# Moving small attention products between the runs of an attention and SwiGLU kernel, sharing row copies between two engines, and taking a statistic in steps

## The chip, the cores and the metric

The kernel runs on one core of one Trainium2 chip. The metric is the device time of one execution in microseconds (us), the median of several. A core has a matrix engine (TensorE, PE in the profile, with its weight loads shown apart as PEld), a vector engine (VectorE, DVE), an activation engine (ScalarE, ACT), a general engine (GpSimd, POOL), and a sync engine (SyncE, SP) that here only issues DMAs. Each engine runs its own instructions in order and waits for others by semaphores. PE writes to accumulators in PSUM, eight banks here, each a tile of 128 x 512 numbers of 32 bits; DVE and ACT read them, POOL doesn't.

## The reference

A linear attention without softmax for 8 batches, 8 heads, 576 rows and 64 columns per head, then a SwiGLU network on its 4608 rows of 512:

```python
kv = einsum('bhsd,bhse->bhde', k, v)              # 64 x 64 per batch and head
o = einsum('bhsd,bhde->bhse', q, kv)
o = o / sqrt(mean(o * o, -1) + 1e-6) * g_norm
x = o.transpose(0, 2, 1, 3).reshape(B * S, H * D)  # 4608 x 512
xn = x / sqrt(mean(x * x, -1) + 1e-6) * rms_g
g, val = xn @ w_gate, xn @ w_val                   # 512 -> 1536
out = (silu(g) * val) @ w_out                      # 1536 -> 512
```

Inputs and output are 32-bit floats; the kernel multiplies in bfloat16 and accumulates in 32 bits.

## The kernel before, in words

The rows are cut into nine groups of 512. Groups 0 to 7 are the first 512 rows of batches 0 to 7. Group 8 holds the remainders, the last 64 rows of each of the eight batches. Groups go through the network in the order 0 to 6, 8, 7.

A group g from 1 on takes 40 slots. The first 24 alternate a gate (`gate_of`) and a value (`val_of`) for each of 12 blocks of hidden units: four multiplies of 512 columns each into a tile of the PSUM pool mm1 (`mm1`, L762). ACT takes the silu of the gate (L771), DVE multiplies it by the value (L783). The last 16 slots are the output multiplies (L811), three in each, into the pool o2; ACT copies the sums (L831) and SP stores them. Pools: mm1 has 3 tiles, o2 has 2, att has 3. A new tile waits until the last reader of its predecessor in the same bank is done.

While PE does the network of one group, the attention of the next batch is placed between its slots. For batch b this is `place_attention`, in the slots of group b - 1. It has a run of k-v products (`kv_mm`, L294, 40 multiplies on 128 rows by 64 columns of the array, into one tile of att), two DVE copies into `kvs` (`kv_half`, L324), and a run of o (`o_heads`, L422, 32 multiplies on 64 rows by 128 columns, into two tiles of o2 and two of att). ACT takes squares and copies of o (`sq_`, `outa_`), POOL weights the squares with g_norm (`wsq`, L514), DVE sums them (`red`, L522), computes the scale per row and head in a chain of 12 small instructions (`chain`), and applies it (`xna_`). SP then turns the result into the layout of x with two transposing DMAs (`x_dma`, L653).

K-v products of 4 and 5 share one run, and those of 6 and 7 (`mate`). The remainders' o comes in pairs of batches (`o_rem`, L397, 16 multiplies on quarters of the array, 64 by 64): batches 0 and 1 in the run of o of batch 2, 2 and 3 with 3, 4 and 5 with 5, 6 and 7 with 7. It is written to half a tile of att and half a tile of mm1, read by four ACT instructions 256 wide (`sq_rem` L405, `outa_rem` L410), goes through the same chain as the fifth chunk, and its transposing DMA fills a part of `xr`, the x of group 8.

Where an operation goes is decided when the program is made. `Placer.put` gives each operation the first slot that its inputs and the engine's estimated backlog allow: `ROOM` is what an engine has free in a slot, `BEHIND` how far it may fall back, and costs are written at each call. `Placer.psum` adds that the tiles of att used before have been read. `start` and `chain_at` are slots that an operation may not precede. In a slot the operations of other engines are issued first, then the slot's own work, then the placed PE operations. The order of the tiles fixed there decides what each engine queues behind what.

Batches 0 and 1 are written out by hand. Batch 0 has no work to hide in: group 0 starts with the first 256 of its rows. `early` lists its slots (gates 0 to 2, then values 0 to 2, gates 3 to 5, values 3 to 5, gates 6 to 8, values 6 to 8), and `behind(n)` what follows slot n for the last 256 rows. `behind(4)` issues products of values 0 to 2 that had been held back (`held`); `behind(9)`, after value 5, has eight PE transposes (L621) and four copies of their rows to x on ACT (`xT_out`, L631; the DVE form of the same copy is L633). The first gate over the last 256 rows is the slot after gate 8. Batch 1 is in `place_second`: four transposed products of k-v with q (`oT_mm`, L472) into att, their squares on ACT (`sqT_`, L483), and sixteen small multiplies that sum the squares over a head (`stat_mm`, L507), which a DVE chain reads (`lead_chain`, L539 and on).

POOL issues the loads of k and v, which cast to bfloat16 on the way (`load_cast`): per batch and tensor a main piece (L200) and a remainder (L196). Batch 2's are the last of a long line behind the weights. SP issues the loads of q from batch 2 on, and the transposing DMAs of q (`qT_dma`).

Of the kernel before, what the change touches and what calls it, by code (L numbers as in the profile page):

```python
# [87 lines left out]
def kernel(  # L88
# [12 lines left out]
    nc = tc.nc  # L101
# [25 lines left out]
    xna_p = pool("xna", 2)  # L127
    x_p = pool("x", 3)
# [30 lines left out]
    q01r = consts.tile([2 * REM, H, D], BF16, name="q01r")  # L159
# [29 lines left out]
    def load_cast(b, t, heads=None):  # L189
        to = qc if t == 0 else (vc if t == 2 else kc)[b % 2]  # L190
        if heads is None:
            if t == 0:
                to = q01r[b * REM : (b + 1) * REM]
            else:
                to = to[:REM, :, NC * D :]
            return nc.gpsimd.dma_start(  # L196
                out=to, in_=src[t][b, :, MAIN:S, :].rearrange("h p d -> p h d")
            )
        view = src[t][b, :, 0:MAIN, :].rearrange("h (p c) d -> p h (c d)", c=NC)[:, heads[0] : heads[1]]
        return nc.gpsimd.dma_start(out=to[:, heads[0] : heads[1], : NC * D], in_=view)  # L200
# [62 lines left out]
    class Att:  # L263
        def __init__(self, b):
            self.b = b
            self.kv, self.qT = kvs[b % 2 if b else 2], qTs[b % 2]
            self.chunks = NC + (b == 2 or b > 2 and b % 2)
            if b < 2:
                self.qTj = self.qT.rearrange("p c j t -> p (c j t)").rearrange("p (j c t) -> p j c t", j=NS, c=NC + 1)
# [51 lines left out]

        def kv_half(self, half):
            rows, cols = slice(half * D, (half + 1) * D), slice(half * D, (half + 1) * D)
            nc.vector.tensor_copy(out=self.kv[rows, :, half, :], in_=self.kv_ps[rows, :, cols])  # L324
# [54 lines left out]
        def qT_dma(self):  # L379
            flat = mains[self.b, 0].rearrange("p c h d -> p (c h d)")  # L380
            nc.sync.dma_start_transpose(out=self.qT[:, 0:NC].rearrange("p c j t -> p (c j) t"), in_=flat)
            if self.chunks > NC:
                rem = q01r if self.b == 2 else rems[0][self.b // 2 % 2]
                nc.sync.dma_start_transpose(out=self.qT[:, NC], in_=rem.rearrange("p h d -> p (h d)"))

        def o_rem(self):

            of = (kvs[2], kvs[1]) if self.b == 2 else (kvs[0], kvs[1])
            self.o[NC] = [
                pool_.tile([128, H // 2, D], FP32, name=name) for pool_, name in ((att_p, "att"), (mm1_p, "mm1"))  # L390
            ]
            for j in range(NS):
                for n in range(2):
                    at = slice(n * REM, (n + 1) * REM)
                    for half in range(2):
                        rows = slice(half * D, (half + 1) * D)
                        nc.tensor.matmul(  # L397
                            self.o[NC][half][at, j, :], lhsT=self.qTj[rows, j, NC, at],
                            rhs=of[n][rows, j, half, :], start=True, stop=True, skip_group_check=True,
                        )  # L400

        def sq_rem(self, half):
            if NC not in self.sq:
                self.sq[NC] = sq_p.tile([128, 2, H, D], BF16, name="sq")
            nc.scalar.activation(out=self.sq[NC][:, 0, half:H:2, :], in_=self.o[NC][half], func=ACT.Square)  # L405

        def outa_rem(self, half):
            if NC not in self.outa:
                self.outa[NC] = outa_p.tile([128, H, D], BF16, name="outa")
            nc.scalar.copy(out=self.outa[NC][:, half:H:2, :], in_=self.o[NC][half])  # L410

        def o_heads(self):
# [5 lines left out]
            for c in range(NC):  # L418
                for j in range(NS):
                    for half in range(2):  # L420
# [3 lines left out]
                            rhs=self.kv[rows, j, half, :], start=True, stop=True, skip_group_check=True,  # L424
# [4 lines left out]
        def part(self, t, n):  # L429

            if n >= NC:
                return t[:, n]
# [12 lines left out]
        def xna_pairs(self, o, js, c0, c1):  # L445
            if not hasattr(self, "xna"):
                self.xna = xna_p.tile([128, NC + 1, H, D], BF16, name="xna")
# [6 lines left out]
        def o_of(self, c):  # L454
            return self.o[c] if c >= NC else self.o["main", c].rearrange("p c h d -> p (c h) d")
# [47 lines left out]
        def stat_mm(self, c0, c1):  # L503
            self.st = st = att_p.tile([128, 2, NC + 1, H], FP32, name="att")
            for c in range(c0, c1):
                for j in range(NS):
                    nc.tensor.matmul(  # L507
                        st[:, :, c, 2 * j : 2 * j + 2], lhsT=self.sqT[:, j, c], rhs=sel,
                        start=c == c0 and j == 0, stop=c == c1 - 1 and j == NS - 1,
                        skip_group_check=True,  # L510
                    )

# [3 lines left out]
        def red(self, c, which):  # L516
            if self.st is None:
                self.st = stat.tile([128, 2, NC + 1, H], FP32, name="st")
            of = self.sq[c][:, which]
            if c < NC:  # L520
                of = of.rearrange("p (c h) d -> p c h d", c=2)
            nc.vector.reduce_sum(out=self.part(self.st[:, which], c), in_=of, axis=AX.X)  # L522

        def chain_t(self):
            if not hasattr(self, "al"):
                t = lambda n, dt=FP32, h=H: stat.tile([128, NC + 1, h], dt, name=n)
                self.u, self.r, self.t, self.z, self.nt, self.al = (t(n) for n in ("u", "r", "t", "z", "nt", "al"))
                self.s = stat.tile([128, NC + 1], FP32, name="srow")
# [57 lines left out]
        def xna_(self, c, eng):  # L586
            if not hasattr(self, "xna"):
                self.xna = xna_p.tile([128, NC + 1, H, D], BF16, name="xna")
            if c < NC:
                of = self.o["main", c] if self.b == 1 else self.outa[c].rearrange("p (c h) d -> p c h d", c=2)  # L590
                return eng.tensor_tensor(  # L591
                    out=self.part(self.xna, c), in0=of,
                    in1=self.part(self.al, c).to_broadcast([128, 2, H // 2, D]), op=OP.mult,
                )
            return eng.tensor_tensor(
                out=self.xna[:, c], in0=self.outa[c], in1=self.al[:, c, :].to_broadcast([128, H, D]), op=OP.mult
# [48 lines left out]
        def x_dma(self, c0, c1):  # L645
# [3 lines left out]
            else:  # L649
                b = self.b // 2 * 2 if self.b > 2 else 0  # L650
                to = xr[:, :, b * REM : (b + 2) * REM]
                of = self.xna[:, NC].rearrange("p h d -> p (h d)")
# [16 lines left out]
    def place_attention(P, b, casts=(), at=0, chain_at=0, mate=None):  # L669
# [3 lines left out]
        N1 = range(a.chunks)  # L673
        P.floor = max(P.floor, at)
        load = P.put("SP", 0.0, a.qT_dma, casts[:1] if b == 2 else casts)
        qt = [("DMA", load[1] + QT_SLOTS)]
        if kv is None:
            of = [a] + ([Att(mate)] if mate else [])
            p = P.psum(1.2, lambda: [o.kv_mm(ALL) for o in of], casts, len(of))
            out_ = [[P.put("DVE", 0.4, lambda o=o, h=h: o.kv_half(h), [p]) for h in range(2)] for o in of]  # L680
            for tile_, ops in zip(P.tiles[-len(of) :], out_):
                tile_ += ops
            kv = out_[0]
            if mate:
                ahead[mate] = of[1], out_[1]
        else:
            P.floor = max(P.floor, start + 2)
        outs, reds = {}, []
        rem = a.chunks - NC
        main = P.psum(0.73 + 0.25 * rem, a.o_heads, kv + qt, 2 + rem)  # L690
        for c in (*N1[NC:], *N1[:NC]):
            if c == NC:
                for n in (1, 0):
# [433 lines left out]
```

## Time and profile before

| What | Value |
|---|---|
| Median of 3 runs | 317.47 us (317.18 to 317.76) |
| The profiled execution's own time | 317.45 us |
| Its span | 315.7 us |
| PE busy | 310.6 us (98%) |
| DVE busy | 167.6 us (53%) |
| ACT busy | 139.1 us (44%) |
| POOL busy | 87.4 us (28%) |
| DMA | 40.18 MB, mean 127 GB/s |

The span runs from the first to the last instruction of the profiled execution; the 1.75 us around it belong to its own time. Times in a profile are from the start of the span. Lines of groups name the line of the kernel, the engine, the operation, output and inputs with shapes, count, busy time and mean ns of one. The chain that ended last is followed back from the last instruction: each piece has a start, a length and what it was. A line of the timeline has a start, a length, the engine, the operation, a count, and in brackets how long the engine had been idle and what ended that; consecutive instructions of one kind are merged. The length of a PE instruction includes the pipeline, so the next starts before it ends; the step from one start to the next is what it costs.

### The profile page before, as it was taken

To read this page: it belongs to the slowest core of one execution; us is meant where nothing else is said; L and a number is where in the kernel's file an instruction comes from. 1 tells how busy PE (TensorE), PEld (TensorE's weight loads), DVE (VectorE), ACT (ScalarE), POOL (GpSimd) and SP (SyncE) were. 2 spreads that over 40 slices of the span, in tenths; PEclk is the share of its full clock that TensorE was granted. 3 is DMA by queue.
4 is the path that set the end of the run, shared out by engine and by line. 5 is a ranking of instruction groups with operands and counts; after the bars stand their busy time and mean duration, and the time that the engine had idled before them with its cause. 6 is when DMAs were issued, how large, how long until landed. Compare 5 with 4: busy or idle time off the path is not lost.

```text
span 315.7 us, 5706 instructions
## 1 busy us (share of the span) xinstructions
PE 310.6 (98%) x2220; PEld 154.8 (49%) x2220; DVE 167.6 (53%) x375; ACT 139.1 (44%) x261; POOL 87.4 (28%) x108
## 2 busy tenths in 40 slices
PE   8999999999999999999999999999999999999996
PEld 3688655544444445444444454444444444444444
DVE  4585456579669643955196638570769034103410
ACT  2374474595487324632483228322842233233321
POOL 8846430077068205830081007100510000000000
PEclk9999999999999999999999999999999999999999
DMA  9999999999899968997423444424001600040002
GB/s 199 194 203 199 196 237 200 192 231 147 190 162 215 179 152 140 253 175 163 166 85 67 94 135 141 83 48 152 3 0 25 194 1 0 21 105 9 2 33 100
DMA packets 78358, 40.18 MB, mean 127 GB/s; under 512 B 43000, under 2 KB 73852, under 8 KB 78332
## 3 DMA queue, kind: packets, MB, share of 16 engines
q0 software_dynamic: 32304, 14.75, 36.5%
q1 hardware_dynamic: 45328, 24.48, 31.6%
q10 hardware_dynamic: 700, 0.59, 0.6%
q8 instruction: 17, 0.28, 0.3%
q14 instruction: 9, 0.07, 0.1%
HBM read 37.78 MB, written 9.44 MB: 150 GB/s over the span
## 4 chain that ended last, share of the span: by engine, by line
PE 94%; DMA 2%; DVE 1%; POOL 1%; issue 1%; ACT 0%; DVEq 0%; POOLq 0%
PE mm L762 58%; PE o L811 27%; DMA vc<-in_v_dram 2%; PE mm L811 2%; PE att L294 2%; PE o L422 1%; PE o L842 1%; PE att L422 1%; PE att L472 1%; DVE h L783 0%; PE att L621 0%; PE mm L804 0%; PE o L762 0%; PE att L397 0%; PE mm L312 0%
## 5 line engine op out<-in xcount | busy, mean ns | idle before, releaser
L783 DVE TENSOR_TENSOR h<-silu,mm 128x512 bf16<-128x512 bf16 (+1 forms) x114 | 73.9, 650 | 101.1 <-PE mm L762 92.4
L771 ACT ACTIVATE silu<-mm 128x512 bf16<-128x512 f32 (+1 forms) x115 | 65.1, 570 | 83.5 <-PE mm L762 73.1
L762 PE MATMUL mm<-x,wv 128*128 128x512 bf16 (+1 forms) x408 | 97.7, 364 | 0.0
L762 PE MATMUL mm<-x,wg 128*128 128x512 bf16 (+1 forms) x404 | 97.5, 364 | 0.1
L811 PE MATMUL o<-wo,h 128*128 128x512 bf16 x396 | 89.6, 379 | 0.0
L762 PEld LDWEIGHTS <-wv 128*128 128x128 bf16 x468 | 45.1, 98 | 46.2
L762 PEld LDWEIGHTS <-wg 128*128 128x128 bf16 x456 | 44.4, 98 | 47.5 <-issue 0.4
L811 PEld LDWEIGHTS <-h 128*128 128x128 bf16 x420 | 40.6, 98 | 47.6
L514 POOL TENSOR_TENSOR sq<-sq,g 128x512 bf16<-128x512 bf16 x28 | 32.0, 1155 | 99.1 <-ACT sq L405 67.4
L831 ACT COPY osb<-o 128x512 f32<-128x512 f32 x33 | 19.3, 587 | 68.7 <-PE o L811 66.7
L522 DVE TENSOR_REDUCE st<-sq 128x8 f32<-128x512 bf16 x56 | 35.9, 678 | 0.0
L591 DVE TENSOR_TENSOR xna<-outa,al 128x512 bf16<-128x512 bf16 x24 | 15.1, 684 | 0.0
L324 DVE CAST kvs<-att 64x256 bf16<-64x256 f32 x14 | 5.9, 422 | 16.8 <-PE att L294 16.6
L200 POOL DMA_DIRECT2D kc<-in_k_dram x7 | 6.5, 924 | 29.0 <-PE att L294 26.1
L762 PE MATMUL mm<-xr,wg 128*128 128x512 bf16 x48 | 12.3, 379 | 0.0
L762 PE MATMUL mm<-xr,wv 128*128 128x512 bf16 x48 | 12.3, 379 | 0.0
L229 POOL CAST main_q<-stg 128x1024 bf16<-128x1024 f32 x10 | 10.1, 1043 | 1.2 <-DMA stg<-in_q_dram 1.2
L929 ACT ACTIVATE wv<-wv,gain 128x384 bf16<-128x384 bf16 x16 | 9.0, 607 | 0.4 <-PE mm L762 0.4
L200 POOL DMA_DIRECT2D vc<-in_v_dram x10 | 8.5, 857 | 2.1 <-PE att L294 1.1
L258 PE MATMUL mm<-idle 128*128 128x512 bf16 x20 | 7.2, 533 | 1.2 <-DVE idle L138 1.2
L811 PE MATMUL mm<-wo,h 128*128 128x512 bf16 x24 | 7.6, 379 | 0.0
L459 ACT ACTIVATE sq<-att 128x512 bf16<-128x512 f32 x12 | 7.5, 626 | 0.0
(151 smaller groups left out, 190.1 us busy)
## 6 DMA issues: line engine op xcount, KB each, us to landing
out_dram<-osb SPq DMA_DIRECT2D x27, 256.0 KB, 2.5
stg<-in_q_dram SPq DMA_DIRECT2D x6, 1024.0 KB, 11.2
vc<-in_v_dram POOLq DMA_DIRECT2D x7, 512.0 KB, 13.1
kc<-in_k_dram POOLq DMA_DIRECT2D x7, 512.0 KB, 7.8
out_dram<-osb SPq DMA_DIRECT2D x17, 128.0 KB, 2.4
wg<-in_moe_w_gate_dram POOLq DMA_DIRECT2D x4, 384.0 KB, 10.1
wv<-in_moe_w_val_dram POOLq DMA_DIRECT2D x4, 384.0 KB, 11.3
wo<-in_moe_w_out_dram POOLq DMA_DIRECT2D x4, 384.0 KB, 14.4
```

Source lines behind the costliest of these rows:

```text
L200: return nc.gpsimd.dma_start(out=to[:, heads[0] : heads[1], : NC * D], in_=view)
L229: return copy(out=mains[b, t][:, cs[0] : cs[1], h0:h1, :], in_=staged[b, t].rearrange("p h (c d) -> p c h d", c=NC)[:, cs[0] : cs[1], h0:h ...
L459: nc.scalar.activation(out=self.sq[c][:, 0], in_=self.o_of(c), func=ACT.Square)
L514: eng.tensor_tensor(out=self.sq[c][:, 1], in0=self.sq[c][:, 0], in1=g2, op=OP.mult)
L522: nc.vector.reduce_sum(out=self.part(self.st[:, which], c), in_=of, axis=AX.X)
L591: return eng.tensor_tensor(out=self.part(self.xna, c), in0=of, in1=self.part(self.al, c).to_broadcast([128, 2, H // 2, D]), op=OP.mult,)
L762: nc.tensor.matmul(ps[:, : c1 - c0], lhsT=w[n][:, s, jj * 128 : (jj + 1) * 128], rhs=x_of(g, s, c0, c1), start=s == 0, stop=s == NS - 1)
L771: nc.scalar.activation(out=sis[g, j][:, c0:c1], in_=ps, func=ACT.Silu)
L783: nc.vector.tensor_tensor(out=hs[g, j][:, c0:c1], in0=sis[g, j][:, c0:c1], in1=v_ps, op=OP.mult)
L811: nc.tensor.matmul(ps, lhsT=hs[g, j][:, t * 128 : (t + 1) * 128], rhs=wo[j // OB][:, j % OB, :], start=j == 0, stop=j == NF - 1)
L831: (eng.copy if eng is nc.scalar else eng.tensor_copy)(out=o, in_=ps)
L929: A.mul(out=w[:, s], in_=w[:, s], mul=gain[:, s : s + 1])
```

## The change

- Batch 0: gate 7 of the first 256 rows takes its tile from o2, not mm1. Of the four row copies in `behind(9)`, the last two go to DVE.
- Batch 1: `stat_mm` is gone. Its sixteen multiplies are four calls of `stat_pairs`, one for each transposed product, in the slots s + 3, s + 4, s + 4 and s + 5; all were in s + 5. Their tile is taken at s + 3.
- K-v: each batch has its own `kvs` tile (from batch 2 on without the zero blocks), and one memset on POOL is dropped. Batch 4's products have a run of their own; those of batch 5 follow o of 4 in its run; those of 6 and 7 follow o of 5 in its run, 6 into att and 7 into mm1.
- Remainders: their q is transposed when it was, but each pair has a tile `qTr` of its own. Their o is computed two pairs at a time: pairs (0, 1) and (2, 3) in the run of o of batch 6, (4, 5) and (6, 7) in that of 7. A tile of att and one of mm1 then hold both pairs, and the squares and copies on ACT are 512 wide, as for the main rows. In batches 6 and 7 the chain is done twice, for the main rows and the remainders (batch 7: remainders first).

The diff, cut to its core:

```diff
-    kvs = [consts.tile([128, NS, 2, D], BF16, name=f"kvs{n}") for n in range(3)]
-    qTs = [consts.tile([128, NC + 1, NS, 128], BF16, name=f"qTs{n}") for n in range(2)]
+    kvs = [consts.tile([128, NS, 2, D] if n < 2 else [128, NS, D], BF16, name=f"kvs{n}") for n in range(B)]
+    qTs = [consts.tile([128, NC, NS, 128], BF16, name=f"qTs{n}") for n in range(2)]
+    qTr = [consts.tile([128, NS, 128], BF16, name=f"qTr{n}") for n in range(B // 2)]
...
-            self.kv, self.qT = kvs[b % 2 if b else 2], qTs[b % 2]
-            self.chunks = NC + (b == 2 or b > 2 and b % 2)
+            self.kv, self.qT = kvs[b], qTs[b % 2]
+            self.rems = {6: (0, 1), 7: (2, 3)}.get(b, ())
+            self.chunks = NC + len(self.rems)
...
-        def kv_mm(self, js):
+        def kv_mm(self, js, pool=None):
             if not hasattr(self, "kv_ps"):
-                self.kv_ps = att_p.tile([128, NS, 2 * D], FP32, name="att")
+                self.kv_ps = (pool or att_p).tile([128, NS, 2 * D], FP32, name="mm1" if pool is mm1_p else "att")
...
         def o_rem(self):
-            of = (kvs[2], kvs[1]) if self.b == 2 else (kvs[0], kvs[1])
-            self.o[NC] = [
-                pool_.tile([128, H // 2, D], FP32, name=name) for pool_, name in ((att_p, "att"), (mm1_p, "mm1"))
-            ]
...
+            for half, (pool_, name) in enumerate(((att_p, "att"), (mm1_p, "mm1"))):
+                self.o["main", NC + half] = pool_.tile([128, 2, H // 2, D], FP32, name=name)
+            for i, r in enumerate(self.rems):
+                for j in range(NS):
+                    for n in range(2):
+                        at = slice(n * REM, (n + 1) * REM)
+                        for half in range(2):
+                            rows = slice(half * D, (half + 1) * D)
+                            nc.tensor.matmul(
+                                self.o["main", NC + half][at, i, j, :], lhsT=qTr[r][rows, j, at],
+                                rhs=Att(2 * r + n).kv_of(rows, j, half), start=True, stop=True, skip_group_check=True,
+                            )
...
-    def place_attention(P, b, casts=(), at=0, chain_at=0, mate=None):
+    def place_attention(P, b, casts=(), at=0, chain_at=0, mates=()):
...
-            of = [a] + ([Att(mate)] if mate else [])
-            p = P.psum(1.2, lambda: [o.kv_mm(ALL) for o in of], casts, len(of))
...
+            p = P.psum(0.85, lambda: a.kv_mm(ALL), casts)
+            kv = halves(a, p)
+            P.tiles[-1] += kv
         else:
             P.floor = max(P.floor, start + 2)
...
-        main = P.psum(0.73 + 0.25 * rem, a.o_heads, kv + qt, 2 + rem)
...
+        def products():
+            a.o_heads()
+            for o, pool_ in zip(of, (None, mm1_p)):
+                o.kv_mm(ALL, pool_)
...
+        main = P.psum(0.73 + 0.25 * len(a.rems) + 0.65 * len(of), products, kv + qt, 2 + rem + bool(of))
+        for n in reversed(range(len(of))):
+            ahead[mates[n]] = of[n], halves(of[n], main)
...
+        for c in (*reversed(range(NC, a.chunks)), *range(NC)):
+            s = P.put("ACT", 0.6, lambda c=c: a.sq_(c), [main])
+            outs[c] = P.put("ACT", 0.6, lambda c=c: a.outa_(c), [main])
...
+        mains, rests = (0, NC), (NC, a.chunks)
+        for c0, c1 in (rests, mains) if b == B - 1 else (mains, rests)[: 1 + rem]:
+            prev = [r for c in range(c0, c1) for r in reds[c]]
+            for n in range(0, 13, 4):
+                prev = [P.put("DVE", 0.8, lambda n=n, c0=c0, c1=c1: [f() for f in a.chain(c0, c1)[n : n + 4]], prev, chain_at)]
+            xn = {c: P.put("DVE", 0.68, lambda c=c: a.xna_(c, V), prev + [outs[c]]) for c in range(c0, c1)}
...
-        P.at("PE", 0.5, lambda: a.stat_mm(0, NC), s + 5)
+        for j in range(NS):
+            P.at("PE", 0.11, lambda j=j: a.stat_pairs((j,), 0, NC, att_p, "att"), s + (3, 4, 4, 5)[j])
...
-        silu_of(g, j, mm1(g, wg, j, c0, c1, "o2" if g == 0 and c0 == 0 and j == 5 else "mm1"), c0, c1)
+        silu_of(g, j, mm1(g, wg, j, c0, c1, "o2" if g == 0 and c0 == 0 and j in (5, 7) else "mm1"), c0, c1)
...
-    G.memset(kvs[0], 0.0)
     G.memset(kvs[1], 0.0)
...
-                    a.xT_out(j, (2, 3), A)
+                    a.xT_out(j, (2, 3), A if js is P0 else V)
...
-            end = place_attention(P, b, casts, s0 - 2, s0 + 2 * NF - 4, b + 1 if b in (4, 6) else None)
+            end = place_attention(P, b, casts, s0 - 2, s0 + 2 * NF - 4, {4: (5,), 5: (6, 7)}.get(b, ()))
```

More of the change, by code (lines that the diff above doesn't have):

```diff
@@ L127 @@
     xna_p = pool("xna", 2)
+    rna_p = pool("rna", 1)
     x_p = pool("x", 3)
@@ L501, in stat_pairs @@
                     first = False
[L503 to L511, printed above, removed]
         def wsq(self, c, eng):
@@ L676, in place_attention, with halves @@
         qt = [("DMA", load[1] + QT_SLOTS)]
+        def halves(o, p):
+            return [P.put("DVE", 0.4, lambda o=o, h=h: o.kv_half(h), [p]) for h in range(2)]
         if kv is None:
[L678 to L682 removed]
@@ new lines, in place_attention @@
+        ends = {}
+        mains, rests = (0, NC), (NC, a.chunks)
[4 more added lines that the diff above has]
+            xn = {c: P.put("DVE", 0.68, lambda c=c: a.xna_(c, V), prev + [outs[c]]) for c in range(c0, c1)}
+            for c in range(c0, c1, 2):
+                for at_ in ((c, c + 2),) if c < NC else ((c, c + 1), (c + 1, c + 2)):
+                    ends[c] = P.put("SP", 0.0, lambda at_=at_: a.x_dma(*at_), [xn[c + 1]])[1]
@@ L713, in place_second @@
+        return ends[NC if b == B - 1 else 2] + X_SLOTS
     def place_second(P, s):
```

108 lines of the change are left out of this document (37 added, 71 removed).

## The prediction, made before the changed kernel was run

> **What bounds the kernel now.** I read the page first (shares of the span, then the chain that ended last), then the timeline engine by engine at each place the change touches, then the landings of the loads there.
>
> ```profile
> span 315.7 us, 5706 instructions
> ...
> PE 310.6 (98%) x2220; PEld 154.8 (49%) x2220; DVE 167.6 (53%) x375; ACT 139.1 (44%) x261; POOL 87.4 (28%) x108
> ...
> PE 94%; DMA 2%; DVE 1%; POOL 1%; issue 1%; ACT 0%; DVEq 0%; POOLq 0%
> ```
>
> PE carries 94% of the chain. No multiply of the network is added or removed, so a saving can only be a wait of PE, or the time PE loses around a change of shape. Behind the start-up, where PE feeds itself dummies, I found waits at two places. The first, in order: PE, its weight loads, DVE, ACT.
>
> ```profile
> 22.43 0.61 PE L621 MATMUL att<-ident,xna 128*128 128x128 bf16 x8
> 23.04 0.60 PE L762 MATMUL mm<-x,wg 128*128 128x256 bf16 x4
> ...
> 23.70 0.86 PEld L762 LDWEIGHTS <-wg 128*128 128x128 bf16 x8 [0.24 <-issue]
> 24.75 0.31 PEld L762 LDWEIGHTS <-wg 128*128 128x128 bf16 x3 [0.19 <-issue]
> ...
> 22.57 0.41 DVE L783 TENSOR_TENSOR h<-silu,mm 128x256 bf16<-128x256 bf16 x1
> ...
> 23.23 0.74 DVE L783 TENSOR_TENSOR h<-silu,mm 128x256 bf16<-128x256 bf16 x2
> 23.89 0.41 DVE L783 TENSOR_TENSOR h<-silu,o 128x256 bf16<-128x256 bf16 x1
> ...
> 22.86 1.57 ACT L631 ACTIVATE x<-att,gain 128x256 bf16<-128x256 bf16 x4 [1.15 <-PE att L621]
> 24.30 0.95 ACT L771 ACTIVATE silu<-mm 128x256 bf16<-128x256 f32 x3
> ```
>
> Here PE waits for accumulators of the pool mm1. Eight transposes from 22.43 end at 22.88 (0.056 each); gate 6 starts at 23.04, 0.05 after the product of value 1 has freed its tile (22.57 + 0.41 = 22.98). Gate 6 ends at 23.47 (4 x 0.109); gate 7 starts at 23.70, after the product of value 3 (23.23 + 0.41). Gate 8 follows at once and ends at 24.57; the next gate, of the second half of the rows, starts at 24.75, after the silu of gate 6 (24.30 + 0.40), which stood behind four row copies on ACT. Waits: 0.16, 0.23 and 0.18.
>
> The second place is the statistics of batch 1, with the row copies of DVE that I use as a price:
>
> ```profile
> 44.05 0.68 PE L507 MATMUL att<-sel,sqT 128*128 128x4 bf16 x16
> ...
> 43.60 0.60 ACT L483 ACTIVATE sqT<-att 128x512 bf16<-128x512 f32 x1 [0.27 <-PE att L472]
> ...
> 49.17 0.60 DVE L633 TENSOR_SCALAR x<-att,gain 128x256 bf16<-128x256 bf16 x2
> ```
>
> The sixteen take 0.54 to the next multiply, of which 16 x 0.026 = 0.42 is work. The fourth needs the last square, done at 43.60 + 0.60 = 44.20: a wait of 0.13.
>
> Third, runs of other shapes: the timeline at k-v of batch 2, then the chain.
>
> ```profile
> 58.03 0.38 PE L762 MATMUL mm<-x,wg 128*128 128x512 bf16 x1
> 58.34 0.35 PE L294 MATMUL att<-vc,kc 128*64 128x64 bf16 x10
> ...
> 58.41 0.75 PE att L294 x40
> ...
> 119.18 1.39 PE att L294 x80
> ```
>
> From one start to the next is 0.31 where a 512-wide multiply takes 0.216 (4.32 for 20 in the chain): 0.10 for the change of shape. Forty take 0.75 alone, eighty 1.39, so a second k-v in a run saves 0.11.
>
> **Part by part, in the order of PE.**
>
> *Rows of batch 0.* Gate 7 goes from mm1 to o2, where the product of value 0 freed a tile at 22.65. It starts at 23.47, not 23.70; gate 8 takes the tile of value 3 (free 23.70) at 23.90; the next gate can take the tile of value 4, free at 23.23 + 0.33 + 0.41 + 0.05 = 24.03, at 24.34. The first wait, 0.16, stays. But two of the four row copies now stand on DVE behind the six products. The last product starts at 23.89; the next instruction follows 0.33 later as between products, at 24.23. DVE's copy takes 0.34 and the pair 0.60, so they end at 24.57 and 24.83 and release PE 0.05 later. The gate needs them as its third and fourth steps: start 24.34, third at 24.62, fourth at 24.88, end 24.99. Before it ended at 24.75 + 0.43 = 25.18. Gain 0.20: two waits of 0.41 go and one of 0.21 comes, DVE being late next. Bounds: 0.41 if DVE hid the copies, 0 if the pair were as slow as on ACT (1.57 / 4 = 0.36 apart and 0.47 long). I take the 0.20, by DVE's own row. ACT's next silus come earlier and no tile waits for them.
>
> *Statistics of batch 1 in four steps.* The same sixteen, four behind each square. The first three squares (41.66 to 43.33, back to back) are done before their turn; the last transposed product starts 0.10 later, its square ends at about 44.30, and PE comes to the last step at 44.35. Gain 0.13 (between 0.05 and 0.13). The statistics' tile now stands between transposed products in the pool att. If an o tile waits for it, that wait ends when DVE has read it, about 45.45, against the start of o near 45.85: nothing.
>
> *One memset less on POOL (0.55).* Behind it POOL waits for landings of loads; nothing.
>
> *K-v of batch 2 against its load.* PE is now 0.20 + 0.13 = 0.33 earlier at 58.34. The last piece of that batch's v:
>
> ```profile
> 42.46 0.69 POOL L196 DMA_DIRECT2D vc<-in_v_dram  x1 [1.53 <-DMA wo<-in_moe_w_out_dram]
> ...
> DMA to landing us min/median/max: 15.8/15.8/15.8
> ```
>
> It lands at 42.46 + 15.8 = 58.27, a time set by the DMA queues and not by PE: the page shows their engines 9 tenths busy up to there, and the change moves no byte of it. The ninth multiply of the run needs it, at 58.34 + 8 x 0.016 = 58.47 before, 0.15 to 0.20 after the landing; now at 58.14. It waits till about 58.31, so of the 0.33 only 0.16 passes. Bounds of this wait: 0 if the piece lands 0.2 earlier in other executions, 0.33 if it lands 0.2 later. I take 0.17.
>
> *Runs from batch 2 on.* Changes of shape before: 2 each for k-v of 2, of 3, of 4 with 5, of 6 with 7, and o of 4 and 6; 3 each for o of 2, 3, 5, 7 with a remainder: 24. After: 2 each for k-v of 2, 3, 4 and o of 2, 3; 3 each for o of 4 with k-v of 5, o of 5 with k-v of 6 and 7, o of 6 and 7 with two remainders: 22. Gain 2 x 0.10 = 0.20. No row shows the change from o's shape to k-v's; with the nearest (other narrow shapes in a row, also 0.10) it is counted at 0.10; free it would give 0.20 more, at double 0.20 less.
>
> *Tiles, ACT and DVE in the later stages.* Remainders in pairs make ACT's instructions 512 wide: 8 of 0.6 for 16 of 0.38, but in two stages only (4 x 0.6 more each than o alone). I cost them at nothing, because a silu has slack: with three mm1 tiles, a tile written at T is asked for again 1.7 later. The last remainder tile was free after two ACT instructions (0.65), now 1.1 after the run (0.48 apart plus 0.6). K-v of 7 in mm1 is freed by two DVE copies of 0.42, some 1.05 after the run. Both are under 1.7. DVE has 12 reductions, not 8 or 10, before the chain's due slot (products and reductions are 0.60 apart, three to a pair of slots: 1.79 against 1.73 of PE, so it falls back by 0.06 per pair, for one pair more). The second chain (12 instructions of about 0.2) and two results fit in the output slots, where DVE has no products. POOL has six products of 1.16 per stage for four or five, early in it. On SP two transposes more per stage (1.2 each) stand before stores, and nobody waits for those. Batch 7 does its remainders first: the piece of xr that landed at 248.92 for a start at 250.18 comes earlier. The k-v loads of 6 and 7 land by 143, o of 5 is at 155.7.
>
> **Sum.** -0.20 - 0.13 + 0.17 - 0.20 = -0.36 us. Against the profiled execution's 317.45 (span 315.7 and 1.75 around it; 0.02 under the median of 317.47) that is **317.1**. About 0.2% (0.63 us) is what a measurement of this kernel can tell from no change, so I expect a gain too small to be told.
>
> **Rivals.**
> *The load is no obstacle.* Then -0.53, or 316.9; with o to k-v free, 316.7. For it: the landing may shift by 0.2. Against: it was under 0.2 ahead of its use. By the Trainium skill, DMA: Bandwidth & Descriptors, Anatomy of one DMA (SWDGE path), a load takes about 2.0 us plus bytes / 436e3; a piece of 64 KB would then be in after 2.2 us, and the sum would be 316.9. The trace has 15.8, and decides.
> *DVE's copies are no faster than ACT's.* Then the gate ends at 24.23 + 0.36 + 0.47 + 0.05 + 0.11 = 25.22 for 25.18: nothing is won there, the load costs nothing (0.07 of slack is left), and the sum is +0.04 - 0.13 - 0.20 = -0.29, 317.2. The Trainium skill, VectorE: DVE Perf Modes, Specifications, says that VectorE sits closer to SBUF and ScalarE closer to PSUM, which speaks against moving these reads. The rows say the opposite: 0.34 on DVE, 0.47 on ACT.
> *Slower: PE waits for mm1 behind the wider remainders.* The place is the first slots behind o of 6 and 7. It decides when ACT and DVE together hold a tile longer than 1.7: ACT's 2.4 of remainders then stand wholly before a silu, and each of the two stages loses up to 2.4 - 1.5 = 0.9 more than before. 2 x 0.9 - 0.36 = +1.4, or 318.9. For it: those activations are indeed put ahead of a silu. Against: the planner allows ACT 0.9 of backlog per slot, and with four instructions (1.5) ahead no wait of PE is to be seen.
> *Nothing comes through:* other executions already wait for the load, and the tails of the changes are hidden: 317.3 to 317.5.
>
> **Numbers.** My forecast (316.8 to 317.4) 0.5; no obstacle 0.22; DVE slow 0.05; nothing 0.1; slower 0.13. Half of the second and a little of the first lie under 316.83: faster 0.25. The slower rival and a little besides: 0.15. Within 0.2%: 0.6. Leaving out a tenth at each end, the range is 316.6 to 317.9.
>
> **What would show it.** Right: gates 7, 8 and the next without a hole up to 24.45, then two short holes behind DVE's row copies; no hole inside the statistics; k-v of 2 with a hole before its ninth multiply at about 58.3; o with k-v some 0.1 under the sum of the separate runs. Wrong: a hole of PE after 150, an mm multiply released by ACT's remainder lines or by k-v's copies, a later landing of v of batch 2, or a start of the remainders' stage behind a transpose.

## The result, and the profile after

The changed kernel takes **316.9 us** (median; 316.44 to 317.52) against 317.49 us (317.01 to 317.99) for the kernel before, run beside it. The ratio is 0.9981, with a 95% interval of 0.9974 to 0.9988. That is 0.59 us less, between 0.38 and 0.83. The prediction took 0.2% for what a measurement can tell from no change, and expected a gain too small to be told. The gain is indeed of that size, but it is told from none: the interval leaves out 1. The forecast of 317.1 was 0.2 too high. The time came out at 316.9, which is what the rival "the load is no obstacle" gave, though not by that rival's terms, as shown below. The profiled execution took 317.07 us, of which 315.3 are its span.

The page of the kernel after, shares of the span and of the chain:

```profile
span 315.3 us, 5721 instructions
...
PE 310.2 (98%) x2220; PEld 154.8 (49%) x2220; DVE 172.7 (55%) x401; ACT 137.7 (44%) x251; POOL 86.8 (28%) x107
...
PE 95%; DMA 2%; POOL 1%; issue 1%; DVE 0%; ACT 0%; DVEq 0%; POOLq 0%
```

PE is still all of the chain that matters. DVE's share of the chain has gone from 1% to 0%: less of PE's time stands behind DVE. ACT has ten instructions fewer and DVE has 26 more, and neither shows in the chain.

The timeline at the rows of batch 0 (start, length, engine, operation, count, idle time before):

```profile
22.75 0.61 PE L601 MATMUL att<-ident,xna 128*128 128x128 bf16 x8
23.20 0.60 PE L753 MATMUL mm<-x,wg 128*128 128x256 bf16 x4
23.64 0.60 PE L753 MATMUL o<-x,wg 128*128 128x256 bf16 x4
24.07 1.24 PE L753 MATMUL mm<-x,wg 128*128 128x256 bf16 x8
25.16 0.49 PE L753 MATMUL mm<-x,wv 128*128 128x256 bf16 x3
...
23.17 0.84 ACT L611 ACTIVATE x<-att,gain 128x256 bf16<-128x256 bf16 x2 [1.15 <-PE att L601]
...
24.06 0.41 DVE L774 TENSOR_TENSOR h<-silu,o 128x256 bf16<-128x256 bf16 x1
24.39 0.60 DVE L613 TENSOR_SCALAR x<-att,gain 128x256 bf16<-128x256 bf16 x2
```

Gates 6, 7 and 8 now start 0.44 apart (23.20, 23.64, 24.07), which is 4 x 0.109, and gate 6 follows the eight transposes at once (22.75 + 8 x 0.056 = 23.20). So the wait of gate 7, 0.23 before, is gone. The wait of gate 6, which the prediction kept at 0.16, is gone too, and that isn't the change's doing (see the two more profiles of the kernel before). The eight multiplies from 24.07 are gate 8 and the next gate. They take until 25.16, 1.09 instead of 8 x 0.109 = 0.87. The starts of the trace put the missing 0.21 in two holes of 0.06 and 0.15, before the third and the fourth step of that gate, each just behind the end of one of DVE's two row copies. The prediction's times for the same steps (24.34, 24.62, 24.88) put them at 0.06 and 0.15 too.

The statistics of batch 1, same view:

```profile
42.51 0.24 PE L491 MATMUL att<-sel,sqT 128*128 128x4 bf16 x4
...
43.47 0.34 PE L491 MATMUL att<-sel,sqT 128*128 128x4 bf16 x8
...
44.32 0.25 PE L491 MATMUL att<-sel,sqT 128*128 128x4 bf16 x4
44.44 0.59 PE L802 MATMUL o<-wo,h 128*128 128x512 bf16 x2
...
43.67 0.60 ACT L477 ACTIVATE sqT<-att 128x512 bf16<-128x512 f32 x1 [0.37 <-PE att L466]
```

The last square ends at 43.67 + 0.60 = 44.27 and the last four multiplies start at 44.32: no hole is left. The next multiply follows 0.12 behind.

K-v of batch 2 and the last v piece that it needs (timeline; the load's group; PE's list of waits, with total, times and longest):

```profile
57.45 0.81 PE L753 MATMUL mm<-x,wg 128*128 128x512 bf16 x3
58.19 0.82 PE L296 MATMUL att<-vc,kc 128*64 128x64 bf16 x40
58.94 0.61 PE L753 MATMUL mm<-x,wv 128*128 128x512 bf16 x2
...
L197 POOL DMA_DIRECT2D vc<-in_v_dram x1: 692/692/692, 43.1 to 43.1; - x1
...
DMA to landing us min/median/max: 14.3/14.3/14.3
...
PE mm L259 <- DVE idle L139: 1.2, 1, 1.2
PE att L340 <- DMA main_q<-in_q_dram: 0.3, 1, 0.3
PE o L601 <- DVE xna L443: 0.2, 1, 0.2
PE mm L314 <- DMA vc<-in_v_dram: 0.2, 1, 0.2
```

Here the forecast failed. The run from 58.19 has all forty multiplies in one line: no hole before the ninth. The piece landed at 43.1 + 14.3 = 57.4, 0.9 ahead of its use at 58.34, where the forecast had the landing at 58.27. PE's list of waits has only start-up entries.

The chain at a run of o with k-v of the next batch, and at the run of o of 7 with two pairs of remainders:

```profile
121.76 0.34 PE o L418 x16
122.10 0.23 PE att L418 x16
122.33 0.75 PE att L296 x40
123.09 19.10 PE mm L753 x88
...
220.41 0.34 PE o L418 x16
220.75 0.23 PE att L418 x16
220.99 0.14 PE att L403
...
221.36 18.24 PE mm L753 x84
```

Each run is followed by a long stretch of network multiplies without a break (88 and 84 of them). Nothing after 62 us makes PE wait.

To compare executions that start up differently, I use four intervals from one start to another on PE, from the starts in the trace:

| Interval | Before, three executions | After |
|---|---|---|
| Lead: first gate of batch 0 to first value over its last 256 rows | 8.746, 8.746, 9.352 | 8.407 |
| Statistics: turn of q of batch 1 to its o | 7.652, 7.652, 7.651 | 7.529 |
| o of batch 1 to k-v of batch 2 | 12.362, 12.360, 12.362 | 12.361 |
| Rest: k-v of batch 2 to the last multiply | 254.006, 254.003, 254.006 | 253.770 |

The second and third executions of the kernel before are the last experiment's. The rest and the statistics repeat within 0.003. The lead is of two kinds. In some executions PE comes from the first gate to the eight transposes without a wait, and these begin 6.00 us behind it; the first gate follows DVE's chain, and I call these executions paced by DVE. The first two of before and the one of after are such. In others PE waits on the way for landings of the network's weights and resumes 0.04 to 0.05 after them, and the transposes begin 6.2 to 6.7 us behind the first gate; I call these paced by the weights. The third of before is one. Among executions paced by DVE the differences are -0.339 - 0.123 - 0.236 = -0.70.

### The profile page after: what moved, and what is told of

Same layout as the page of the kernel before. It is cut to its first block, busy times and chain, and to the rows that moved or that the text cites. A ratio compares the mean times of both kernels' runs of the same rounds, so it can differ in the third digit from the quotient of the medians.

```text
span 315.3 us, 5721 instructions
## 1 busy us (share of the span) xinstructions
PE 310.2 (98%) x2220; PEld 154.8 (49%) x2220; DVE 172.7 (55%) x401; ACT 137.7 (44%) x251; POOL 86.8 (28%) x107
## 4 chain that ended last, share of the span: by engine, by line
PE 95%; DMA 2%; POOL 1%; issue 1%; DVE 0%; ACT 0%; DVEq 0%; POOLq 0%
PE mm L753 58%; PE o L802 27%; DMA vc<-in_v_dram 2%; PE mm L802 2%; PE att L296 1%; PE o L418 1%; PE o L833 1%; PE o L753 1%; PE att L418 1%; PE att L466 1%; PE att L601 0%; PE mm L795 0%; PE mm L314 0%; POOL vc L201 0%; POOL remv L899 0%
## 5 line engine op out<-in xcount | busy, mean ns | idle before, releaser
L574 DVE TENSOR_TENSOR xna<-outa,al 128x512 bf16<-128x512 bf16 x24 | 15.1, 684 | 0.0
L330 DVE CAST kvs<-att 64x256 bf16<-64x256 f32 x12 | 5.1, 421 | 13.3 <-PE att L296 13.2
L453 ACT ACTIVATE sq<-att 128x512 bf16<-128x512 f32 x14 | 8.6, 615 | 0.0
L457 ACT CAST outa<-att 128x512 bf16<-128x512 f32 x14 | 8.4, 602 | 0.0
```

The lines of the kernel that those rows point to most:

```text
L453: nc.scalar.activation(out=self.sq[c][:, 0], in_=self.o_of(c), func=ACT.Square)
L574: return eng.tensor_tensor(out=self.part(self.xna, c) if c < NC else self.part(self.rna, c - NC), in0=of, in1=self.part(self.al, c).to_bro ...
```

## The experiments

**The runs alone.** The lead and the statistics are put back; k-v, o and the remainders stay as in the kernel after.

```diff
-        for j in range(NS):
-            P.at("PE", 0.11, lambda j=j: a.stat_pairs((j,), 0, NC, att_p, "att"), s + (3, 4, 4, 5)[j])
+        P.at("PE", 0.5, lambda: a.stat_mm(0, NC), s + 5)
...
-        silu_of(..., "o2" if g == 0 and c0 == 0 and j in (5, 7) else "mm1"), c0, c1)
+        silu_of(..., "o2" if g == 0 and c0 == 0 and j == 5 else "mm1"), c0, c1)
...
-                    a.xT_out(j, (2, 3), A if js is P0 else V)
+                    a.xT_out(j, (2, 3), A)
```

> The changed kernel with its first two parts undone: gate 7 back in mm1, all four row copies on ACT, and the sixteen statistics multiplies together again; only the moved k-v and remainder runs are left. My theory (the runs save two changes of shape and two short tails, nothing else): from the first multiply of k-v of batch 2 to the last multiply 253.99 us as in the changed kernel, against 254.23 before, so -0.24 us in all, about 317.25; the early stretches as before, 8.75 us from the first gate of batch 0 to the first value over the last 256 rows, and 7.65 us from the turn of q of batch 1 to its o. Rival (the moved runs are worth nothing, the gain is all in the start): 254.2 us for the last stretch, and the time of before, 317.5.

It took 317.47 us (316.76 to 318.24) beside 317.63 for the kernel before: ratio 0.9991, interval 0.9976 to 1.0007. By itself that can't be told from no change. The intervals can be (the expectation's 253.99 and 254.23 stand 0.22 above the table's figures for the same two kernels, so their difference is what counts): lead 8.751 and statistics 7.654, as before, and the rest 253.768, as after. So the runs are worth 254.00 - 253.77 = 0.24, and the other two parts the remainder of the gain. The last v piece was 0.84 ahead of its use here.

**The row copies all on ACT**, with gate 7 still in o2.

```diff
-                    a.xT_out(j, (2, 3), A if js is P0 else V)
+                    a.xT_out(j, (2, 3), A)
```

> The changed kernel with all four row copies on ACT again; gate 7 stays in o2. If gate 7's tile is what PE gains by, the next gate starts right after gate 8, has no hole inside, and the following value waits for the silu of gate 6, which stands behind four copies again (free at about 24.75 where batch 0's first gate starts at 16.44): 8.3 us from the first gate to that value, and the gate after it waits 0.1 more for the silu of gate 8, so 8.86 us to there, where the changed kernel has 8.84 and the one before 9.18. If the sharing of the copies is what PE gains by, it is the 9.18 of before.

317.11 us beside 317.63, ratio 0.9977 (0.9963 to 0.9992). This profile was paced by DVE. The lead is 8.310, and to the gate after it 8.857; after has 8.407 and 8.841, before 9.183 to the same place. The timeline of this kernel:

```profile
23.78 0.60 PE L753 MATMUL o<-x,wg 128*128 128x256 bf16 x4
24.22 1.04 PE L753 MATMUL mm<-x,wg 128*128 128x256 bf16 x8
25.19 0.60 PE L753 MATMUL mm<-x,wv 128*128 128x256 bf16 x4
25.74 0.49 PE L753 MATMUL mm<-x,wg 128*128 128x256 bf16 x3
```

The first value starts 0.10 later than eight unbroken steps would allow (25.19 against 24.22 + 0.87), and the next gate 0.11 later than four (25.74 against 25.19 + 0.44). PE waits as long as in the kernel after, one gate later, for silus behind the four copies. So in an execution paced by DVE the tile in o2 alone makes nearly all of the lead's gain, and sharing the copies adds 0.02 (8.857 - 8.841).

**Gate 7 back in mm1**, with the row copies shared.

```diff
-        silu_of(..., "o2" if g == 0 and c0 == 0 and j in (5, 7) else "mm1"), c0, c1)
+        silu_of(..., "o2" if g == 0 and c0 == 0 and j == 5 else "mm1"), c0, c1)
```

> The changed kernel with gate 7 back in mm1; two row copies stay on DVE. By the prediction's own sum, DVE's two copies behind the six products set the end of the stretch, whatever gate 7 does: gate 7 waits 0.24 for the product of value 3 again, the two holes behind the copies are gone, and the first gate to the first value over the last rows takes 8.42 us, the 8.41 of the changed kernel. If the tile of gate 7 is needed for the gain, 8.6 us or more.

316.80 us beside 317.63, ratio 0.9972 (0.9957 to 0.9988): no slower than after. The timeline shows why this profile doesn't answer the question:

```profile
22.33 0.61 PE L601 MATMUL att<-ident,xna 128*128 128x128 bf16 x8
22.95 1.92 PE L753 MATMUL mm<-x,wg 128*128 128x256 bf16 x16
24.71 0.60 PE L753 MATMUL mm<-x,wv 128*128 128x256 bf16 x4
```

Four gates in a row, 16 x 0.109 = 1.75, without any hole, though three of them share mm1's tiles. In this execution PE had been kept late by the weights: it resumed 0.04 to 0.05 after the landings of the first and second pieces of the value weights and the third piece of the gate weights (17.42, 20.97 and 22.91), so gate 6 stands 0.17 behind the transposes, and DVE's products were all done when PE came. The lead was 9.101, yet from gate 6 to the first value it took only 1.758. The last v piece of batch 2 landed at 57.85, in the middle of its range, but PE was early: it came to the ninth multiply at 57.89, and the run of k-v took 0.650 instead of 0.626. It is the only execution of this schedule in which the load cost anything.

> The kernel with gate 7 back in mm1 once more, because in its first profile PE waited for weights in the first 23 us. If batch 0's v lands at 11 us or later, so that DVE's chain and not the weights set the pace: a wait of some 0.24 before gate 7, hardly any hole behind it, and 8.42 us from the first gate to the first value over the last rows. If it lands earlier: waits that end 0.05 after the landings of the weights, and 1.75 us without a hole from gate 6 to that value.

The second profile, of 316.40 us, was paced by the weights as well (lead 8.591, gate 6 to first value 1.758), and the k-v run took 0.626 again. So where the weights set the pace, sharing the copies leaves no hole even with gate 7 in mm1. What gate 7's tile is worth in this kernel where DVE sets the pace wasn't seen in either.

**The product of value 5 behind DVE's row copies.**

```diff
-        if leads and j < FB[0]:
+        if leads and (j < FB[0] or j == 5):
...
                     a.xT_out(j, (2, 3), A if js is P0 else V)
+            held.pop(5)()
```

> The changed kernel with the product of value 5 held back until the two row copies are issued on DVE. If DVE's queue is what is left of the waits there, both holes (0.06 and 0.15) go, 8.19 us from the first gate to the first value over the last rows for 8.41, and 0.2 us less in all: about 316.7, against 316.9 of the changed kernel. If the holes are not DVE's queue (a copy in itself late by its input or its tile), they stay, 8.41 and 316.9.

316.91 us (316.53 to 317.33) beside 317.63, ratio 0.9976 (0.9964 to 0.9988). This profile was paced by the weights too: lead 9.038, gate 6 to first value 1.756.

> The kernel with the product of value 5 behind the row copies once more, for the same reason. With v of batch 0 at 11 us or later: 8.19 us from the first gate to the first value over the last rows, no hole behind gate 8. With an earlier landing: PE waits for weights up to gate 6, and 1.75 us from there.

This second profile was paced by DVE, with a lead of 8.268, the shortest of all. The timeline of weight loads shows the two holes of the kernel after gone:

```profile
23.59 1.76 PEld L753 LDWEIGHTS <-wg 128*128 128x128 bf16 x16
25.36 0.32 PEld L753 LDWEIGHTS <-wv 128*128 128x128 bf16 x3
```

Gates 6, 7, 8 and the next run at 0.11 a step, gate 6 to first value in 1.744, against 1.953 in the kernel after. The mechanism is as expected. The lead is 8.268 and not 8.19 because a small DVE instruction of batch 0's statistics took 244 ns for some 175, which put gate 6 0.07 later. In time the 0.2 can't be told: the ratio of 0.9976 against the kernel before stands beside the 0.9981 of the kernel after, well within both intervals, and the profiles paced by the weights don't have the holes. I found no version that clearly beats the kernel after.

**K-v of batch 2 two slots earlier.** This makes PE ask for the load before it can have landed, which tells a load that is out of the way from one that sets a wall.

```diff
-            return [op, ("DMA", at + 12)]
+            return [op, ("DMA", at + 10)]
```

> The changed kernel with the k-v run of batch 2 two slots earlier, at about 56.5 us. The term of the prediction that failed said that its last piece of v holds PE. If that piece is a wall in time, at 57.4 to 58.3 as in the six profiles so far, PE stops in this run: its first multiply waits some 0.4 for the main piece (landed at 56.5 to 57.0) and its ninth 0.9 to 1.2 for the remainder, the run takes 1.5 to 2 us for 0.63, and the time is some 1.2 us over that of the changed kernel, about 318.1. If the loads come when they are asked for, or PE doesn't wait for them, the run takes 0.63 and the time is that of the changed kernel.

318.35 us (318.23 to 318.84) beside 317.37 for the kernel before: ratio 1.0033 (1.0020 to 1.0046), the only kernel slower than before. Its timeline and PE's longest wait:

```profile
55.35 1.03 PE L753 MATMUL mm<-x,wg 128*128 128x512 bf16 x4
56.88 0.32 PE L296 MATMUL att<-vc,kc 128*64 128x64 bf16 x8 [0.50 <-DMA vc<-in_v_dram]
57.99 0.70 PE L296 MATMUL att<-vc,kc 128*64 128x64 bf16 x32 [0.79 <-DMA vc<-in_v_dram]
...
PE att L296 <- DMA vc<-in_v_dram: 1.3, 2, 0.8
```

PE is held twice: before the first multiply for the main piece, and before the ninth for the last piece, which landed at 42.8 + 15.1 = 57.9. Counted from start to start, PE lost 0.57 and 0.98, or 1.55 together. The time is 0.98 above that of the kernel before, where the kernel after was 0.59 below: 1.57 in all. The landing stayed in the range that it has when PE asks two slots later. So the mechanism that the prediction feared exists, at exactly the multiply that it named, and none of this wait is given back later. In the kernel after it is simply not reached.

**K-v runs joint again**, 4 with 5 and 6 with 7 as before; the remainders stay two pairs at a time.

```diff
-            p = P.psum(0.85, lambda: a.kv_mm(ALL), casts)
+            both = [a] + ([Att(mate)] if mate else [])
+            p = P.psum(1.2 if mate else 0.85, lambda: [o.kv_mm(ALL) for o in both], casts, len(both))
...
-            end = place_attention(..., {4: (5,), 5: (6, 7)}.get(b, ()))
+            end = place_attention(..., (), b + 1 if b in (4, 6) else None)
```

> The changed kernel with the k-v runs as they were before (4 with 5, 6 with 7, each pair in a run of its own in the output slots); the remainders stay two pairs at a time. By my count of changes of shape this has 22 as the changed kernel: from k-v of batch 2 to the last multiply 253.77 us as there, 254.01 before, and the same time, about 316.9. So the moved k-v is worth nothing and the remainders are all of it. Rival (k-v in the run of o saves PE time): 253.9 or more, as one run more is entered and left.

316.86 us (316.35 to 317.47) beside 317.37, ratio 0.9981 (0.9971 to 0.9991), the ratio of the kernel after. Its timeline, and that of its weight loads:

```profile
118.34 1.46 PE L296 MATMUL att<-vc,kc 128*64 128x64 bf16 x80
...
21.33 1.21 PEld L758 LDWEIGHTS <-wv 128*128 128x128 bf16 x12 [0.47 <-DMA wv<-in_moe_w_val_dram]
...
23.27 1.64 PEld L758 LDWEIGHTS <-wg 128*128 128x128 bf16 x16 [0.18 <-DMA wg<-in_moe_w_gate_dram]
```

The eighty stand together again, and the rest takes 253.760, 0.01 less than after. The moved k-v products are therefore worth nothing, and the gain of the runs is all the remainders'. The weight loads show the other kind of start: they wait for landings of the value's and of the gate's weights, and the four gates then run without a hole (gate 6 to first value 1.757).

**The kernel before, two more profiles**, to see what the same start costs without the change.

> The kernel before once more, for what the first part of the change is worth when the loads of the weights set the pace of the first 23 us. If v of batch 0 lands before 10.8 us and gate 6 starts 0.05 after its weights have landed, I expect from gate 6 to the first value over the last rows 1.75 us plus a hole of about 0.2 before the next gate (silu of gate 6 behind four copies), where such profiles of the changed kernel's variants have 1.75. If it lands later: 2.15 as in the first profile.

317.38 us. The lead was 8.746 again, but from gate 6 to the first value it took 2.293, more than either figure expected. V of batch 0 had landed at 10.73, yet PE didn't wait for the weights of gate 6: it followed the transposes at once. Here is one DVE instruction of the profile that the prediction was made from, then the same one, PE and ACT in this profile:

```profile
19.35 0.32 DVE L571 TENSOR_SCALAR y<-z 128x16 int32<-128x16 int32 x1
...
19.27 0.17 DVE L571 TENSOR_SCALAR y<-z 128x16 int32<-128x16 int32 x1
...
22.35 0.61 PE L621 MATMUL att<-ident,xna 128*128 128x128 bf16 x8
22.81 1.70 PE L762 MATMUL mm<-x,wg 128*128 128x256 bf16 x12
24.67 0.60 PE L762 MATMUL mm<-x,wg 128*128 128x256 bf16 x4 [0.16 <-ACT silu L771]
...
22.78 1.57 ACT L631 ACTIVATE x<-att,gain 128x256 bf16<-128x256 bf16 x4 [1.15 <-PE att L621]
24.22 0.95 ACT L771 ACTIVATE silu<-mm 128x256 bf16<-128x256 f32 x3
```

This instruction of batch 0's statistics stands ahead of DVE's products. It took 322 ns in the first profile and 174 here and in the kernel after, and so the products, and gate 6 behind them, came 0.15 later in the first. The gate over the last rows doesn't feel that. In both profiles it waits for the silu of gate 6 (here 24.22 + 0.40, and the gate at 24.67), which stands behind the four copies, and these follow the transposes. So the lead is 8.746 with the slow instruction and without it.

The last v piece landed at 57.56, 0.85 ahead of its use, where it had been 0.22 ahead in the profile that the prediction was made from.

> As the run before, to have both cases: 1.95 us from gate 6 to the first value over the last rows where the weights set the pace, 2.15 to 2.25 where DVE's chain does.

318.19 us. This one was paced by the weights, and took 2.13 from gate 6 to the first value, more than expected:

```profile
23.77 1.49 PE L762 MATMUL mm<-x,wg 128*128 128x256 bf16 x12
25.47 0.60 PE L762 MATMUL mm<-x,wg 128*128 128x256 bf16 x4 [0.21 <-ACT silu L771]
...
23.58 1.57 ACT L631 ACTIVATE x<-att,gain 128x256 bf16<-128x256 bf16 x4 [1.52 <-PE att L621]
25.02 0.95 ACT L771 ACTIVATE silu<-mm 128x256 bf16<-128x256 f32 x3
```

Gates 6, 7 and 8 run without a hole here, as DVE had caught up. But gate 6's silu, at 25.02, still stands behind four row copies on ACT, and the next gate waits for its tile: 25.47 against 23.77 + 12 x 0.109 = 25.08, a hole of 0.38. In the five profiles of variants with shared copies that the weights paced, that hole is gone and the same stretch takes 1.76. So in such an execution the first part of the change is worth 2.13 - 1.76 = 0.37, by one profile of the kernel before, and nearly twice the 0.20 of the forecast.

## Why the prediction was right or wrong

| Step | Predicted | Measured |
|---|---|---|
| Rows of batch 0 | -0.20 | -0.34 (lead, 8.746 to 8.407) where DVE sets the pace; -0.37 (gate 6 to first value, 2.13 to 1.76) where the weights do |
| Statistics of batch 1 | -0.13 | -0.12 |
| K-v of batch 2 against its load | +0.17 | 0 (0.02 in one profile) |
| Runs from batch 2 on | -0.20 | -0.24 |
| Later stages | 0 | 0 |
| Sum | -0.36 | -0.70 by the profiles; -0.59 (-0.83 to -0.38) in time |

The total fell inside the range, but two terms were mis-sized, both on the cautious side: the load and the rows of batch 0. The rival "the load is no obstacle" had the first right, and met 316.9 partly by luck, since its -0.53 holds the same -0.20 for the rows.

**Rows of batch 0: the right mechanism, too small a size.** Gate 7's wait goes and the two short holes come, as forecast. The step that failed is "the first wait, 0.16, stays". That wait came from the one DVE instruction that took 322 ns in the profile at hand. Without it gate 6 starts at once in both kernels. The kernel before gains nothing by that, since its lead ends with the silu behind the copies either way (8.746 in both); in the kernel after, by the prediction's own sum, the end of the stretch hangs on DVE, and is earlier by as much. So the lead falls by 0.34. From gate 6 alone it would seem 0.19 (2.146 to 1.953), but the first of these was cut short by the late gate 6. The prediction also didn't see that a second kind of start exists, with PE behind the weights; there the hole that goes is the silu's.

**DVE's copies** took 0.60 for the pair, as the row of before said, so the rival in which they are no faster than ACT's fell. What sharing them is worth depends on the start. Where DVE sets the pace it is 0.02: with four on ACT the same delay comes one gate later. Where the weights set the pace, sharing alone leaves no hole, by both profiles of the kernel with gate 7 back in mm1; what gate 7's tile alone would do there no run shows.

**Statistics: right.** The hole of 0.13 went, and nothing waited for the tile that is now taken earlier.

**"K-v of batch 2 against its load" is the other step that failed.** Its term was +0.17 and the measured one 0. The reasoning took the landing at 58.27 from one profile, and called it a time set by the queues and not by PE. That much is so, as the two-slot experiment shows. But across the profiles of kernels with the run in its place the landing lies anywhere between 57.4 and 58.3, and the profile of before had the latest. In ten of those eleven the piece was 0.2 to 1.6 ahead of its use, and in the one miss it cost 0.02. PE's own arrival at that multiply moves still more, from 57.66 to 59.21, with the start of the kernel. The prediction had the right multiply, as the two-slot experiment shows, and even the bound of 0; it chose between the bounds by the one row that it had, and that row was an extreme. Of the two estimates of a load, the fit in the Trainium skill (DMA: Bandwidth & Descriptors, Anatomy of one DMA), an estimate of 2.2 us for 64 KB, remains far from the 14.2 to 15.8 us of these traces. I read the difference as time behind the loads queued ahead, as the page of the profile has the DMA engines 9 tenths busy up to there; no run here isolates it. That the fit gave the better sum was a coincidence.

**Runs: right in size, partly for another reason.** The forecast counted changes of shape, 24 to 22, at 0.10 each. Counted from start to start, less the network's own 0.216 a multiply, a remainder pair adds 0.25 to a run of o in the kernel before; in the kernel after the first adds 0.25 and the second 0.126. So two changes into the quarter shape are saved, at 0.25 - 0.126 = 0.12 each: 0.25. K-v behind o costs 0.75 and alone 0.85, so a change is indeed 0.10 between narrow shapes. But splitting the joint runs costs as much as that saves: the k-v products of 4 to 7 take 2.96 before and 2.98 after. The Trainium skill, TensorEngine Tiling (Array Packing), Key Properties, says that a change of tiling mode drains the engine; the traces agree, in that each change costs PE 0.10 to 0.12.

**Slower, by mm1 behind the wider remainders: not seen.** No multiply after 62 us waits for ACT or DVE. The slack that the forecast counted, 1.7 against 1.1, was enough.

What stays open: what gate 7's tile is worth with shared copies where DVE sets the pace, and how often each kind of start occurs. From the first value over the last rows to the end, the span takes 290.50 in all three profiles of the kernel before, and 290.12 to 290.15 in the kernel after and in the four profiles of the two variants that differ from it only before that value (gate 7 back in mm1, the product of value 5 held back). So of the measured 0.59 (0.38 to 0.83) 0.37 is the statistics and the runs, and 0.22 (0.01 to 0.46) is left for the rows of batch 0. The 0.34 to 0.37 of the profiles lies in that, and so does the forecast's 0.20: the time alone can't choose between them.

## What to carry to other kernels

A landing or a release read off one profile is a sample. Before a term of the sum is built on a margin of 0.2 us to a DMA, look at how far that landing, and the engine's own arrival, move between executions, and take the middle of what they do rather than the value at hand. A wait may come from one slow instruction; a second profile of the unchanged kernel tells. Which of two waits ends last can differ between executions, so a gain at the start of a kernel may be worth different amounts in them. Instructions of another array shape are best gathered with others of the same shape: here the second remainder pair of a run cost half of the first, while moving k-v products between runs without saving a change gave nothing.

## What was not expected of the hardware

The start of the kernel moves by more than the change is worth. The first gate began between 15.6 and 17.2 us over the profiles, with the v of batch 0 landing between 10.2 and 11.7; in about half of them PE then followed the landings of the weights up to gate 6, in the others DVE. A late start doesn't cost its whole delay: in two variants of the kernel after, the first gate of one profile was 1.59 us behind that of the other, and the first value over the last rows 0.76, as PE then waited for weights in the early one.

One DVE instruction on a small tile took 174 to 190 ns in most profiles, but 244 in one and 322 in another, with the same shape. The one of 322 is of the kernel before, whose other two profiles have 174 and 175.
